# First layer of an MoE block on scaled fp16 pairs, with weight staging in freed slots and later maxima turns (one core)

## The chip, the cores and the metric

The kernel runs on one core of a Trainium2 chip. The metric is the time of one execution in microseconds (us) on the device. Engines: TensorE (PE) multiplies matrices, VectorE (DVE) and ScalarE (ACT) work elementwise, GpSimd (POOL) helps them, SyncE (SP) issues DMAs; GpSimd issues DMAs too.

## The reference

Causal attention with a bias from a cumulative sum gives x of 2304 tokens by 512; two mixture-of-experts blocks follow (as dense two-layer networks).

```
scores = q @ k.T / 8                       # 4 batches, 8 heads, 576 positions, 64 dims
bias   = min(-(cum_i - cum_j), 0),  cum = cumsum(max(s, 0))
x  = softmax(causal(scores + bias)) @ v    # -> (2304, 512)
h  = x @ moe_w_in                          # 512 x 2048
x  = (h * tanh(softplus(h))) @ moe_w_out   # 2048 x 512
h  = x @ moe2_w_in
out = (h * sigmoid(1.702 h)) @ moe2_w_out
```

## The kernel before

**Numbers in pairs.** A product of two float32 matrices is made of three matmuls (`mm3`): high by high, high by low and low by high part, since each operand is kept as a high part and the remainder. In the first block both parts are of the type fp32r, four bytes wide; in the second block they are fp16, scaled by powers of two.

**Weights.** The weights arrive as 64-bit numbers. For each of the 16 chunks (128 columns) of moe_w_in, `fetch_w` loads 512 KB into a staging tile `wst`; `turn_w` converts it: ScalarE once, VectorE twice (a shift, TENSOR_SCALAR, and a combination, SCALAR_TENSOR_TENSOR, both on 128x512 elements), then ScalarE copies the high part into `w` and GpSimd subtracts to get the low part.

**First layer (`first_layer`, `l1_mm`).** The 2304 tokens go in 9 units of 256 (`u`); each unit takes 16 chunks times 4 slices of 128 rows times 3 products, 192 matmuls of 128x256, into PSUM tile `h` (`acc` in the last two units); ScalarE evicts to `hs`, which goes to DRAM as `h_d`. Seven units are woven between attention steps (`slot_a`, `tick`), the last two stand behind the attention. x reaches this layer through `emit_tile`: TensorE transposes (`xt`), ScalarE writes the high part of `xh`, VectorE the low one.

**Start.** Up to step 6 of the attention the instructions stand in the order of the program (`nc.mode = "strict"`), with three calls of `bg_a` (one weight chunk each) between the scores of steps 3 to 5. Behind that a scheduler orders the instructions of each engine. Each engine then runs its own queue in order; the k, q and v loads stand in GpSimd's queue.

**Second layer.** The second layer of the first block goes over 5 spans of tokens (four of 512, one of 256), 960 matmuls `acc<-gh,w` and `acc<-gl,w`. After every 12 of these of 512 columns one background job (`bg_step`) is issued: passes over the second block's weights on VectorE (`out_pass1`, `out_scale`, `in_pass`, `in_split`, `in_scale`). The fourth span's matmuls are numbers 577 to 768.

**Maxima over the partitions (`across`).** For the scale of a span (`spx`) or of the weights (`gsc`) VectorE spreads a column over a 128x128 tile `bc`, TensorE transposes it into a bank of PSUM (`acc<-ident,bc` in the trace, "turn" below), and VectorE reduces it (`spx<-acc`, `gsc<-acc`). The turn is issued `wait` steps after the column; TensorE's next turn or matmul into the same bank waits for the reduce.

```
soon.append([wait, turn])
...
across(gsc[:, 0:1], out_scale2, 2 * SOON)      # SOON = 7
```

The second block starts at about 697 us, on fp16 pairs.

Of the kernel before, what the change touches and what calls it, by code (L numbers as in the profile page):

```python
# [19 lines left out]
VTOP = 16384.0  # L20
PH = 3
# [14 lines left out]
WAH = 1  # L36
LAG0 = 2
NEAR = 26
FA = 3
# [51 lines left out]
def attention_moe_moe_kernel(  # L91
# [82 lines left out]

    raw = {}
# [122 lines left out]

    vsc, vmx = {}, {}
# [14 lines left out]
    def vscale_set(b):  # L314
# [11 lines left out]
        nc.vector.tensor_scalar(out=t[:, 1:2], in0=t[:, 0:1], scalar1=PSC, scalar2=None, op0=ALU.mult)  # L326
# [287 lines left out]
    def norm_tile(x):  # L614
# [4 lines left out]
        nc.vector.tensor_scalar(out=rs, in0=su, scalar1=1e-9, scalar2=vsc[x["b"]][:, 1:2], op0=ALU.add, op1=ALU.mult)  # L619
# [3 lines left out]
    def emit_tile(x):  # L623
# [114 lines left out]
    I32 = mybir.dt.int32  # L738
# [32 lines left out]
    def turn_w(pool, lay, m, kind):  # L771
        t = pool.tile([128, 2, DM], F32R, tag="w", name="w")
        (win_t if kind == "in" else wout_t)[lay, m] = t
        r = fetched.pop((lay, m, kind))
        th, tl_ = t[:, 0, :], t[:, 1, :]
        if not wide:
            nc.scalar.activation(out=th, in_=r, func=AF.Copy)
            nc.vector.tensor_tensor(out=tl_, in0=r, in1=th, op=ALU.subtract)
            return
        zi, yi = r[:, :, 0], r[:, :, 1]  # L780
        y = yi.bitcast(F32)
        sided = lay == 0 and kind == "in"
# [12 lines left out]
        if lay == 0 and kind == "out":  # L795
            nc.gpsimd.tensor_scalar(out=th, in0=y, scalar1=1.0, scalar2=0.0, op0=ALU.mult, op1=ALU.add)
        else:
            nc.scalar.activation(out=th, in_=y, func=AF.Copy)
# [8 lines left out]
    def l1_mm(ps, lay, m, xr, first):  # L807
        w = win_t[lay, m]
# [7 lines left out]
    wq = list(range(NF))  # L816
# [50 lines left out]
    score(2)  # L867
    early_turn(1, 1)
# [5 lines left out]
    bg_a()  # L874
# [4 lines left out]
    bg_a()  # L879
# [3 lines left out]
    bg_a()  # L883
# [3 lines left out]
    emit_tile(steps[5])  # L887
    nc.mode = "after"
# [31 lines left out]

    def first_layer(u, xr, each):
        for m in range(0, NF, 4):
            t = tmp_pair(F32, "hs")
            for e in range(2):
                ps = ps_h.tile([128, 512], F32, tag="h", name="h")
                for d in range(2):
                    while wq and (0, min(NF - 1, m + 2 * e + d + WAH)) not in win_t:
                        bg_a()
                    while fq and fq[0] <= m + 2 * e + d + WAH + FA:
# [4 lines left out]
                nc.scalar.activation(out=o, in_=ps, func=AF.Copy)  # L934
# [91 lines left out]
    for m in range(NF):  # L1026
# [6 lines left out]
        nc.scalar.activation(out=o, in_=ps, func=AF.Copy)  # L1033
# [22 lines left out]
    def across(col, then, wait=SOON):  # L1056
# [9 lines left out]
        soon.append([wait, turn])  # L1066

    def soon_step():
        for x in soon:
            x[0] -= 1  # L1070
# [44 lines left out]
    def out_scale():  # L1115
        amax(gsc[:, 0:1], wom)
        across(gsc[:, 0:1], out_scale2, 2 * SOON)
# [109 lines left out]
    for i, (u, t0, W, m0, n) in enumerate(groups1):  # L1227
# [24 lines left out]
        if m0 + n == NF:  # L1252
# [3 lines left out]
            def out1(e, acc=acc, k_=k_, mx=mx, u=u, t0=t0, W=W):  # L1256
# [167 lines left out]
```

## Time and profile before

| | us |
|---|---|
| median of 3 runs | 1037.28 (1036.56 to 1040.79) |
| the profiled execution | 1039.73 |
| its span, first to last instruction | 1038.0 |
| TensorE busy | 985.0 (95%) |
| VectorE busy | 689.9 (66%) |
| ScalarE busy | 544.9 (52%) |
| GpSimd busy | 387.2 (37%) |

The span is the profiled execution without 1.7 us around it. Busy shares are means over stages: start to 49.6 us, first dense part to 109, a short part to 134.5 (the last step of batch 0), attention with the first layer to 420.4, second layer of the first block to about 697, then the second block. All instructions that a helper emits carry the line of that helper (L77), so that they are told apart by their tiles.

### The profile page before, as it was taken

The numbers are of one execution on the slowest core, as the hardware profiler recorded it, in microseconds if no ns is written. First come the engines' busy times: TensorE is split into PE (matmuls) and PEld (weight loads), VectorE is DVE, ScalarE is ACT, GpSimd is POOL, SyncE is SP. The second block draws the span as 40 slices with busy tenths as digits, with TensorE's granted clock in tenths as the row PEclk, the third lists the DMA queues.
The fourth block names the chain that finished last, engine by engine and source line by source line (L and its number), as shares of the span: only waits on it lengthen the run. The fifth ranks groups of instructions, "written<-read, shape, count | busy, mean of one in ns | idle before, by whom it ended". The sixth has DMA issues, their size and how long they took to land.

```text
span 1038.0 us, 20212 instructions
## 1 busy us (share of the span) xinstructions
PE 985.0 (95%) x7966; PEld 872.4 (84%) x7970; DVE 689.9 (66%) x1257; ACT 544.9 (52%) x1054; POOL 387.2 (37%) x414
## 2 busy tenths in 40 slices
PE   6799999989989899999996989999999999999997
PEld 5688798879979789998885868988888888888886
DVE  6478677755565775799998984985653653653553
ACT  4476577766665885365655564553433433333331
POOL 2544442243123311586321315575343442342431
PEclk9789999999999999999998999999999999999999
DMA  6458359997699978779996552600110100000000
GB/s 174 107 146 246 102 133 167 221 234 164 138 212 220 171 158 182 271 268 347 339 339 211 201 203 81 203 22 1 41 42 1 39 24 1 21 19 3 21 9 34
DMA packets 153775, 143.17 MB, mean 138 GB/s; under 512 B 91216, under 2 KB 122448, under 8 KB 153680
## 3 DMA queue, kind: packets, MB, share of 16 engines
q1 hardware_dynamic: 147456, 124.05, 43.9%
q0 software_dynamic: 6224, 17.83, 6.7%
q8 instruction: 62, 1.02, 0.4%
q14 instruction: 33, 0.27, 0.1%
HBM read 89.61 MB, written 32.58 MB: 118 GB/s over the span
## 4 chain that ended last, share of the span: by engine, by line
PE 48%; DVE 11%; DMA 10%; issue 3%; ACT 3%; POOL 2%; SPq 1%; DVEq 0%; ACTq 0%; POOLq 0%
PE h L77 24%; PE p L77 16%; DVE wst L77 5%; PE acc L77 4%; PE s L77 2%; DMA wst<-in_moe_w_out_dram 2%; DMA pt<-hl 2%; PE o L77 1%; DMA wst<-in_moe_w_in_dram 1%; DVE gl L77 1%; DMA vraw<-in_v_dram 1%; DMA h_d<-hs 1%; POOL w L77 1%; POOL w2d L77 1%; DMA w2f<-w_d 1%
## 5 line engine op out<-in xcount | busy, mean ns | idle before, releaser
L77 PE MATMUL h<-x,w2i 128*128 128x256 f16 x1728 | 200.0, 273 | 0.0
L77 PE MATMUL acc<-gh,w 128*128 128x512 f32 (+1 forms) x640 | 185.0, 374 | 13.5 <-DVE spx L77 13.5
L77 PE MATMUL h<-xh,w 128*128 128x256 f32 x1344 | 196.6, 295 | 1.1 <-ACT xh L77 0.7
L77 PEld LDWEIGHTS <-w2i 128*128 128x128 f16 x1728 | 169.0, 98 | 19.6
L77 PEld LDWEIGHTS h<-xh,w 128*128 128x128 f32 x1344 | 172.8, 195 | 4.1 <-ACT xh L77 1.1
L77 PEld LDWEIGHTS acc<-gh,w 128*128 128x128 f32 x640 | 117.9, 191 | 35.8 <-DVE spx L77 14.4
L77 PE MATMUL p<-w2h,gl 128*128 128x256 f16 x504 | 135.9, 273 | 1.1 <-DVE gl L77 1.1
L77 PE MATMUL p<-w2l,gh 128*128 128x256 f16 x504 | 136.0, 273 | 0.0
L77 PE MATMUL p<-w2h,gh 128*128 128x256 f16 x504 | 133.4, 273 | 1.1 <-ACT gh L77 0.9
L77 POOL TENSOR_TENSOR s<-z 128x256 f32<-128x256 f32 x72 | 54.7, 780 | 201.8 <-DVE z L77 201.8
L77 PE MATMUL acc<-gl,w 128*128 128x512 f32 (+1 forms) x320 | 119.2, 373 | 0.0
L77 PEld LDWEIGHTS <-gh 128*128 128x128 f16 x1008 | 98.5, 98 | 12.9 <-ACT gh L77 1.2
L77 ACT ACTIVATE sg<-h,spx 128x512 f32<-128x512 f32 x72 | 48.7, 680 | 105.0 <-PE h L77 105.0
L77 DVE TENSOR_TENSOR gl<-z,gh 128x768 f16<-128x768 f32 (+1 forms) x54 | 77.1, 1428 | 34.5 <-ACT gh L77 21.9
L77 DVE SCALAR_TENSOR_TENSOR wst<-wst 128x512 int32<-128x512 int32 x96 | 91.1, 958 | 10.0 <-ACT wst L77 6.6
L77 DVE SCALAR_TENSOR_TENSOR z<-h,sg 128x512 f32<-128x512 f32 x72 | 49.3, 687 | 68.8 <-ACT sg L77 68.7
L77 POOL TENSOR_TENSOR gl<-z,gh 128x1024 fp32r<-128x1024 f32 x18 | 51.0, 2832 | 116.9 <-ACT gh L77 103.8
L77 DVE TENSOR_TENSOR gl<-s,gh 128x1024 f16<-128x1024 f32 x36 | 44.2, 1228 | 68.5 <-ACT gh L77 68.5
L77 ACT ACTIVATE gh<-z 128x1024 fp32r<-128x1024 f32 (+1 forms) x72 | 67.9, 947 | 33.8 <-DVE z L77 29.4
L77 PE MATMUL s<-kw,qw 128*128 128x288 f32 (+4 forms) x352 | 81.8, 339 | 2.4 <-DVE kw L77 2.2
L77 ACT ACTIVATE gh<-s 128x1024 f16<-128x1024 f32 x36 | 38.0, 1057 | 81.7 <-POOL s L77 81.7
L77 ACT ACTIVATE P<-P,mx 128x128 f32<-128x128 f32 (+4 forms) x108 | 62.7, 582 | 19.9 <-DVE mx L77 19.5
(146 smaller groups left out, 1765.2 us busy)
## 6 DMA issues: line engine op xcount, KB each, us to landing
h_d<-hs SPq DMA_DIRECT2D x36, 512.0 KB, 4.4
hg<-h_d SPq DMA_DIRECT2D x36, 512.0 KB, 6.4
wst<-in_moe_w_in_dram SPq DMA_DIRECT2D x32, 512.0 KB, 5.3
wst<-in_moe_w_out_dram SPq DMA_DIRECT2D x32, 512.0 KB, 5.4
ck<-cum_d SPq DMA_DIRECT2D x6, 768.0 KB, 7.8
x_d<-x SPq DMA_DIRECT2D x18, 256.0 KB, 5.2
out_dram<-o SPq DMA_DIRECT2D x9, 512.0 KB, 2.8
kraw<-in_k_dram POOLq DMA_DIRECT2D x32, 128.0 KB, 4.1
```

Of the source, the lines that this page charges most:

```text
L77: r = f(*a, **kw)
```

## The change

The change has three parts.

First, the first layer's operands become scaled fp16 pairs. Two neighbouring chunks make a pair. `pair_a` converts both and takes their peaks on VectorE (`wmx`); `pair_b` makes one bound for the pair: `bound` spreads the peaks over the partitions by a TensorE matmul with ones into a tile `bd`, and VectorE reduces it, clamps, inverts and cuts it to a power of two (`wk`), with its inverse in `isw`. ScalarE writes the scaled high part, and VectorE (no longer GpSimd) the low part. x of batch 0 is scaled by a bound from the peaks of v (`v_peak`, `x_scale`); for later batches the power of two of v's scale stays in x. `evict` multiplies by the inverse scales in ScalarE's copy; at the borders of two batches (units 2, 4 and 6) it takes two copies in place of one, 24 more in all.

Second, chunks are staged in free slots of the 16 slots that the finished weights use (8 pairs, 8 stages), and fetched six chunks ahead (`FA`), no longer three.

Third, the turns of `out_scale` and of spans 0 to 2 are issued at steps 57, 59, 60 and 65 of a clock that counts all steps (`soon_step`), in place of 14 steps behind their columns. Of the 960 matmuls, 384, 468, 576, 732 and 768 stood in TensorE's queue ahead of the five turns before; now 648, 672, 694, 732 and 753 do, which is in the fourth span. The second and the later ones write into the bank that the turn ahead of them used.

```diff
-FA = 3
+FA = 6
...
+    def bound(t, cols, n, tiny, top):
+        ps = ps_s.tile([128, 512], F32, tag="s", name="bd")
+        nc.tensor.matmul(out=ps[:, 0:n], lhsT=ones, rhs=cols, start=True, stop=True, skip_group_check=True)
+        nc.vector.tensor_reduce(out=t, in_=ps[:, 0:n], axis=mybir.AxisListType.X, op=ALU.max)
+        nc.vector.tensor_scalar(out=t, in0=t, scalar1=tiny, scalar2=1.0 / top, op0=ALU.max, op1=ALU.mult)
+        nc.vector.reciprocal(t, t)
+        pow2(t)
...
+    def x_scale(k, ni):
+        for i in range(vmd[0], ni):
+            for g in range(2):
+                v_peak(i, g)
+        vmd[0] = max(vmd[0], ni)
+        sx[k] = t = sm_p.tile([128, 2], F32, tag="sx", name="sx", bufs=3)
+        bound(t[:, 0:1], vm0[:, 0:2 * ni], 2 * ni, 1.0e-30, VTOP)
+        ev_table(k, t)
+
+    def ev_table(k, t):
+        sx[k] = t
+        nc.vector.reciprocal(t[:, 1:2], t[:, 0:1])
...
-                xunit[u] = xh_a.tile([128, 2, KC, U], F32R, tag="xh", name="xh")
+                xunit[u] = xh_a.tile([128, 2, KC, U], F16, tag="xh", name="xh")
             xu = xunit[u]
             src = pv[:, :, done:done + m]
             hi = xu[:, 0, :, off:off + m]
-            nc.scalar.activation(out=hi, in_=src, func=AF.Copy)
-            nc.vector.tensor_tensor(out=xu[:, 1, :, off:off + m], in0=src, in1=hi, op=ALU.subtract)
+            lo = xu[:, 1, :, off:off + m]
+            if b:
+                nc.scalar.activation(out=hi, in_=src, func=AF.Copy)
+                nc.vector.tensor_tensor(out=lo, in0=src, in1=hi, op=ALU.subtract)
+            else:
+                k_ = f"u{u}"
+                if k_ not in sx:
+                    x_scale(k_, min(NTIL, (u + 1) * U // 128))
+                k_ = sx[k_][:, 0:1]
+                nc.scalar.activation(out=hi, in_=src, func=AF.Copy, scale=k_)
+                nc.vector.scalar_tensor_tensor(out=lo, in0=src, scalar=k_, in1=hi, op0=ALU.mult, op1=ALU.subtract)
             done += m
...
-            rt = tmp_pair(F32, "wst")
+            rt = wa_p.tile([128, 1024], F32, tag="w", name="wst")
...
+    def pair_a(p):
+        wmx[p] = t = sm_p.tile([128, 2], BF16, tag="wmx", name="wmx")
+        for m in (2 * p, 2 * p + 1):
+            while fq and fq[0] <= m:
+                fetch_a()
+            r = fetched[0, m, "in"]
+            y = to_f32(r, True) if wide else r
+            fetched[0, m, "in"] = y
+            peak(t[:, m % 2:m % 2 + 1], y)
+
+    def pair_b(p):
+        k = sm_p.tile([128, 1], F32, tag="wk", name="wk")
+        bound(k, wmx.pop(p), 2, TINY, WTOP1)
+        nc.vector.reciprocal(isw[:, p:p + 1], k)
+        win_t[p] = t = wa_p.tile([128, 2, 2, DM], F16, tag="w", name="w")
+        for e in range(2):
+            y = fetched.pop((0, 2 * p + e, "in"))
+            nc.scalar.activation(out=t[:, e, 0, :], in_=y, func=AF.Copy, scale=k)
+            nc.vector.scalar_tensor_tensor(
+                out=t[:, e, 1, :], in0=y, scalar=k, in1=t[:, e, 0, :], op0=ALU.mult, op1=ALU.subtract
+            )
...
+    def pairs_to(pa, pb):
+        for k, f, n in ((1, pair_b, pb), (0, pair_a, pa)):
+            while wq[k] < min(n, NF // 2):
+                f(wq[k])
+                wq[k] += 1
...
     early_pt(steps[2])
     early_av(steps[1])
-    bg_a()
     emit_tile(steps[1])
     score(4)
     early_pt(steps[3])
     early_av(steps[2])
-    bg_a()
+    pairs_to(1, 0)
     score(5)
     early_pt(steps[4])
     early_av(steps[3])
-    bg_a()
+    pairs_to(2, 1)
     early_pt(steps[5])
     early_av(steps[4])
     early_av(steps[5])
     emit_tile(steps[5])
+    pairs_to(2, 2)
...
+    def evict(o, ps, p, t0, t1, n):
+        ov, pv = (x.rearrange("p (d t) -> p d t", d=n) for x in (o, ps))
+        for a, z, k in x_class(t0, t1):
+            e = ev_need(k)[:, p:p + 1]
+            if k == "u0":
+                nc.vector.tensor_tensor(out=e, in0=isw[:, p:p + 1], in1=sx[k][:, 1:2], op=ALU.mult)
+            nc.scalar.activation(
+                out=ov[:, :, a - t0:z - t0], in_=pv[:, :, a - t0:z - t0], func=AF.Copy, scale=e
+            )
...
-                    while wq and (0, min(NF - 1, m + 2 * e + d + WAH)) not in win_t:
-                        bg_a()
-                    while fq and fq[0] <= m + 2 * e + d + WAH + FA:
+                    p = (m + 2 * e) // 2
+                    pairs_to(p + 2, p + 1 + d)
+                    while fq and fq[0] < m + 2 * e + d + FA:
                         fetch_a()
                     l1_mm(ps[:, d * U:(d + 1) * U], 0, m + 2 * e + d, xr, d == 0)
                     each()
                 o = t[:, e * 512:(e + 1) * 512]
-                nc.scalar.activation(out=o, in_=ps, func=AF.Copy)
+                evict(o, ps, m // 2 + e, u * U, (u + 1) * U, 2)
...
-        soon.append([wait, turn])
+        soon.append([wait - (clock[0] if wait > SOON else 0), turn])
+
+    clock = [0]
 
     def soon_step():
+        clock[0] += 1
...
-        across(gsc[:, 0:1], out_scale2, 2 * SOON)
+        across(gsc[:, 0:1], out_scale2, 57)
...
-                        spx[:, u, 0:1], lambda: span_scale(u) if ready[0] else waiting.append(u), 2 * SOON if u < 3 else 99
+                        spx[:, u, 0:1], lambda: span_scale(u) if ready[0] else waiting.append(u), (59, 60, 65, 999, 999)[u]
```

On **VectorE**, in the strict part at the start, before (`p` is a transposed block of probabilities, `x` the attention's output, `mx` and `rs` its maxima and sums):

```order
L77 TENSOR_REDUCE mx<-s 128x2
L77 COPY p_373<-pt 128x512
L77 TENSOR_SCALAR rs<-su 128x4
L77 RECIPROCAL rs<-rs 128x4
L77 TENSOR_TENSOR x<-o,rs 128x256
L77 TENSOR_SCALAR wst<-wst 128x512
L77 SCALAR_TENSOR_TENSOR wst<-wst 128x512
L77 COPY p_394<-pt 128x512
```

The same place after the change, up to the same copy (named p_430 here):

```order
L77 TENSOR_REDUCE wk<-bd 128x1
L77 TENSOR_SCALAR wk<-wk 128x1
L77 RECIPROCAL wk<-wk 128x1
L77 TENSOR_SCALAR wk<-wk 128x1
L77 RECIPROCAL isw<-wk 128x1
L77 SCALAR_TENSOR_TENSOR w<-wst,wk,w 128x512 x2
L77 TENSOR_SCALAR wst<-wst 128x512
L77 SCALAR_TENSOR_TENSOR wst<-wst 128x512
L77 TENSOR_REDUCE wmx<-wst 128x1
L77 TENSOR_SCALAR wst<-wst 128x512
L77 SCALAR_TENSOR_TENSOR wst<-wst 128x512
L77 TENSOR_REDUCE wmx<-wst 128x1
```

Where one conversion stood ahead of the copy, the bound and the low parts of the first pair and the conversion with peaks of the second pair stand now.

On **GpSimd**, the start of its queue, before:

```order
L77 MEMSET cumb 32x576
L77 TENSOR_TENSOR w<-wst,w 128x512 x3
L77 DMA kraw<-in_k_dram 128x4x64
L77 DMA qraw<-in_q_dram 128x4x64
L77 DMA v<-in_v_dram 128x4x64
L77 DMA kraw<-in_k_dram 128x4x64 x2
```

And after the change:

```order
L77 MEMSET cumb 32x576
L77 MEMSET vm_106 128x10
L77 MEMSET ones 128x128
L77 MEMSET maskp 128x64
L77 AFFINE_SELECT maskp<-maskp 64x64 x2
L77 DMA v<-in_v_dram 128x4x64 x4
L77 DMA v<-in_v_dram 64x4x64 x2
L77 DMA kraw<-in_k_dram 128x4x64
```

The three subtractions ahead of the loads are gone, and the v loads have moved ahead of the k loads.

On **VectorE** in the second layer, before, around the reduce of the second turn (`w2i` are the finished weights of the second block, `rk` their scales):

```order
L77 RECIPROCAL rk<-rk 128x1
L77 TENSOR_REDUCE mx_7265<-x_7266 128x1
L77 SCALAR_TENSOR_TENSOR w2i<-wst,rk,w2i 128x512 x2
L77 TENSOR_REDUCE spx<-acc 128x1
L77 SCALAR_TENSOR_TENSOR w2i<-wst,rk,w2i 128x512 x2
```

After the change, around the reduce of the first turn, which is behind the last pass over the weights:

```order
L77 TENSOR_REDUCE gsc<-rk 128x1
L77 SCALAR_TENSOR_TENSOR w2i<-wst,rk,w2i 128x512 x4
L77 COPY bc<-spx 128x128
L77 TENSOR_REDUCE gsc<-acc 128x1
L77 TENSOR_SCALAR gsc<-gsc 128x1
L77 RECIPROCAL gsc<-gsc 128x1
L77 TENSOR_TENSOR gl<-z,gh 128x1024
```

No reduce of a turn stands between the passes any longer; all of them follow the last split.

## Rows read from the trace of the kernel before

**Rows 1.** Busy time of each engine by stretch, with granted clock, DMA share and GB/s.
```profile
49.60:109.00 59.40, 55.72 (x414) 48.99 (x418) 47.27 (x91) 40.71 (x93) 26.80 (x27) 0.94 0.61 182
...
134.50:420.40 285.90, 271.88 (x2611) 247.81 (x2611) 184.50 (x502) 194.93 (x500) 75.53 (x106) 0.99 0.90 187
420.40:628.00 207.60, 194.05 (x988) 165.65 (x987) 191.84 (x259) 120.51 (x159) 87.60 (x49) 0.97 0.77 265
```

**Rows 2.** Timeline of VectorE, TensorE and GpSimd, 32 to 49 us.
```profile
32.77 0.68 DVE L77 COPY p<-pt 128x512 f32<-128x512 f32 x1
...
35.51 0.42 DVE L77 TENSOR_TENSOR x<-o,rs 128x256 f32<-128x256 f32 x1 [1.77 <-PE o L77]
...
37.37 7.47 PE L77 MATMUL h<-xh,w 128*128 128x256 f32 x36 [0.69 <-ACT xh L77]
...
48.75 0.62 PE L77 MATMUL s<-kw,qw 128*128 128x384 f32 x2 [2.16 <-DVE kw L77]
...
34.86 0.90 POOL L77 DMA_DIRECT2D kraw<-in_k_dram  x1
```

**Rows 3.** Groups of VectorE instructions up to 134.5 us (busy, mean ns, idle before).
```profile
L77 DVE SCALAR_TENSOR_TENSOR wst<-wst 128x512 int32<-128x512 int32 x16 | 11.7, 730 | 4.3 <-ACT wst L77 3.8
L77 DVE TENSOR_SCALAR wst<-wst 128x512 int32<-128x512 int32 x16 | 8.5, 533 | 0.1
...
L77 DVE TENSOR_REDUCE mx<-s 128x1 f32<-128x512 f32 x8 | 5.4, 679 | 0.3 <-PE s L77 0.3
...
L77 DVE TENSOR_TENSOR x<-o,rs 128x256 f32<-128x256 f32 x8 | 3.4, 422 | 2.1 <-PE o L77 1.8
...
L77 DVE RECIPROCAL rs<-rs 128x4 f32<-128x4 f32 x9 | 1.6, 173 | 0.2
```

**Rows 4.** VectorE timeline around 32 and 98 us: one step of the conversion.
```profile
31.64 0.42 DVE L77 TENSOR_SCALAR wst<-wst 128x512 int32<-128x512 int32 x1
32.16 0.69 DVE L77 SCALAR_TENSOR_TENSOR wst<-wst 128x512 int32<-128x512 int32 x1
...
98.74 1.19 DVE L77 TENSOR_SCALAR wst<-wst 128x512 int32<-128x512 int32 x1
```

**Rows 5.** Groups of GpSimd instructions up to 134.5 us.
```profile
L77 POOL TENSOR_TENSOR w<-wst,w 128x512 fp32r<-128x512 f32 x16 | 20.8, 1303 | 48.2 <-ACT w L77 47.4 <-issue 0.9
```

**Rows 6.** Chain of waits, 134.5 to 420.4 us: shares, and one piece.
```profile
by line: PE h L77 26.2%; PE s L77 8.8%; DMA pt<-hl 5.7%; PE o L77 5.3%; DMA vraw<-in_v_dram 3.8%; DMA vl<-in_v_dram 2.5%; DMA wst<-in_moe_w_out_dram 2.4%; issue 2.2%; DMA ck<-cum_d 2.2%; SPq L77 2.1%; PE kt L77 1.8%; PE qt L77 1.7%; DVE hl 
...
237.84 8.32 PE h L77 x69
```

**Rows 7.** Chain of waits, 697 to 1038 us: one piece.
```profile
700.58 2.62 PE h L77 x24
```

**Rows 8.** Groups of TensorE instructions, 134.5 to 420.4 us.
```profile
L77 PE MATMUL h<-xh,w 128*128 128x256 f32 x1115 | 158.9, 291 | 0.0
```

**Rows 9.** Groups of TensorE instructions, 420.4 to 628 us.
```profile
L77 PE MATMUL acc<-gh,w 128*128 128x512 f32 x443 | 140.5, 398 | 13.5 <-DVE spx L77 13.5
L77 PE MATMUL acc<-gl,w 128*128 128x512 f32 x221 | 87.6, 396 | 0.0
L77 PE MATMUL acc<-xh,w 128*128 128x256 f32 x321 | 38.7, 283 | 0.0
```

**Rows 10.** Waits of TensorE, 445 to 690 us.
```profile
PE acc L77 <- DVE spx L77: 13.5, 2, 9.6
```

**Rows 11.** The stretch behind the first turn, columns as in the first group.
```profile
561.00:565.75 4.75, 4.59 (x11) 3.63 (x12) 3.46 (x7) 2.02 (x4) 0.00 (x0) 0.50 0.83 251
```

**Rows 12.** VectorE timeline, late part.
```profile
560.82 0.28 DVE L77 TENSOR_REDUCE spx<-acc 128x1 f32<-128x128 f32 x1
...
622.86 4.31 DVE L77 SCALAR_TENSOR_TENSOR w2i<-wst,rk,w2i 128x512 f16<-128x512 f32 x4 [0.70 <-ACT w2i L77]
627.09 1.21 DVE L77 TENSOR_TENSOR gl<-z,gh 128x1024 fp32r<-128x1024 f32 x1
640.87 2.46 DVE L77 TENSOR_TENSOR gl<-z,gh 128x1024 fp32r<-128x1024 f32 x1 [12.56 <-PE acc L77]
```

More of the change, by code (lines that the diff above doesn't have):

```diff
@@ L20 @@
 VTOP = 16384.0
+WTOP1 = 16384.0
 PH = 3
@@ L172, in tmp_pair, with pow2, peak @@
         return p.tile([128, 1024], dt, tag="hs", name=nm)
+    I32 = mybir.dt.int32
+    def pow2(x):
+        nc.vector.tensor_scalar(
+            out=x.bitcast(I32), in0=x.bitcast(I32), scalar1=0x7F800000, scalar2=None, op0=ALU.bitwise_and
+        )
+    ones = const.tile([128, 128], BF16, name="ones")
+    isw = const.tile([128, NF // 2], F32, name="isw")
+    sx, evs = {}, {}
+    def peak(out, in_):
+        nc.vector.tensor_reduce(out=out, in_=in_, axis=mybir.AxisListType.X, op=ALU.max, apply_absolute_value=True)
+    def bound(t, cols, n, tiny, top):
[5 more added lines that the diff above has]
+        pow2(t)
     raw = {}
@@ L297, in split_items, with v_peak, ev_need, x_class @@
         return [qT], [v1, v2] if b else [], kT
+    vm0 = sm_p.tile([128, 2 * NTIL], BF16, tag="vm0", name="vm0", bufs=1)
+    vmd = [0]
+    def v_peak(i, g):
+        n = min(128, S - 128 * i)
+        peak(vm0[:n, 2 * i + g:2 * i + g + 1], vt[0, i, g][:n].rearrange("p h d -> p (h d)"))
+    def x_scale(k, ni):
[9 more added lines that the diff above has]
+        nc.vector.reciprocal(t[:, 1:2], t[:, 0:1])
+    def ev_need(k):
+        if k not in evs:
+            evs[k] = e = const.tile([128, NF // 2], F32, name=f"ev{k}")
+            if k != "u0":
+                nc.vector.tensor_scalar(out=e, in0=isw, scalar1=sx[k][:, 1:2], scalar2=None, op0=ALU.mult)
+        return evs[k]
+    def x_class(t0, t1):
+        r = []
+        while t0 < t1:
+            b = t0 // S
+            m = min(t1, (b + 1) * S)
+            r.append((t0, m, b if b else f"u{t0 // U}"))
+            t0 = m
+        return r
     vsc, vmx = {}, {}
@@ L325, in vscale_set @@
         nc.vector.reciprocal(t[:, 0:1], t[:, 0:1])
-        nc.vector.tensor_scalar(out=t[:, 1:2], in0=t[:, 0:1], scalar1=PSC, scalar2=None, op0=ALU.mult)
+        pow2(t[:, 0:1])
+        ev_table(b, t)
     LK = S // 128 * 128
@@ L618, in norm_tile @@
         su = ts["sums"]
-        nc.vector.tensor_scalar(out=rs, in0=su, scalar1=1e-9, scalar2=vsc[x["b"]][:, 1:2], op0=ALU.add, op1=ALU.mult)
+        nc.vector.tensor_scalar(out=rs, in0=su, scalar1=1e-9, scalar2=PSC, op0=ALU.add, op1=ALU.mult)
         nc.vector.reciprocal(rs, rs)
@@ L769, in fetch_w, with to_f32 @@
         fetched[lay, m, kind] = r
[L771 to L779, printed above, removed]
+    def to_f32(r, sided):
         zi, yi = r[:, :, 0], r[:, :, 1]
         y = yi.bitcast(F32)
-        sided = lay == 0 and kind == "in"
         if sided:
@@ L794, in turn_w @@
             )
[L795 to L798, printed above, removed]
+        return y
+    wmx = {}
+    def pair_a(p):
[18 more added lines that the diff above has]
+            )
+    def turn_w(pool, lay, m, kind):
+        t = pool.tile([128, 2, DM], F32R, tag="w", name="w")
+        wout_t[lay, m] = t
+        r = fetched.pop((lay, m, kind))
+        th, tl_ = t[:, 0, :], t[:, 1, :]
+        if not wide:
+            nc.scalar.activation(out=th, in_=r, func=AF.Copy)
+            nc.vector.tensor_tensor(out=tl_, in0=r, in1=th, op=ALU.subtract)
+            return
+        y = to_f32(r, False)
+        nc.gpsimd.tensor_scalar(out=th, in0=y, scalar1=1.0, scalar2=0.0, op0=ALU.mult, op1=ALU.add)
         nc.gpsimd.tensor_tensor(out=tl_, in0=y, in1=th, op=ALU.subtract)
@@ L815, in attention_moe_moe_kernel @@
     nxt = [0]
-    wq = list(range(NF))
+    wq = [0, 0]
     fq = list(range(NF))
@@ L844, in attention_moe_moe_kernel @@
     nc.gpsimd.memset(cumb[96:128], 0.0)
+    nc.gpsimd.memset(vm0, 0.0)
     nc.vector.tensor_copy(identb, ident)
+    nc.gpsimd.memset(ones, 1.0)
     one = sm_p.tile([128, H], F32, tag="one", name="one", bufs=1)
@@ L867, in attention_moe_moe_kernel @@
     score(2)
+    for i_, g in short:
+        v_peak(i_, g)
+    vmd[0] = 2
     early_turn(1, 1)
@@ L1032, in attention_moe_moe_kernel @@
             l1_mm(ps[:, d * U:(d + 1) * U], 0, m, xl[d], d == 0)
-        nc.scalar.activation(out=o, in_=ps, func=AF.Copy)
+        evict(o, ps, m // 2, (NU - UE) * U, NT, 1)
         if m % 2:
```

15 lines of the change are left out of this document (2 added, 13 removed).

## The prediction

> **What bounds the kernel now.** I read the busy time by stretch first [rows 1]; it shows no single bound. In the dense part from 49.6 to 109 us TensorE is busy 55.72 of 59.4 us, but VectorE has only 12.1 us free there. From 134.5 to 420.4 us TensorE leads (271.88 of 285.9). From 420.4 to 628 us VectorE is busy 191.84 of 207.6 us, and that is the stage where TensorE stands still: the table of waits has 13.5 us in two waits for `spx`, the longest 9.6 [rows 10]. To see whose the end of that stage is, I then followed VectorE's timeline: it goes through the passes over the second block's weights, starts the last split at 622.86 us, does a `gl` at 627.09 us, and then waits 12.56 us for TensorE [rows 12]. So VectorE's chain of passes ends at about 627 us, and from there the matmuls bound.
>
> **The change, step by step.**
>
> *Start, strict part.* Up to the copy of step 5's probabilities at 32.77 us [rows 2] VectorE gets: four peaks of v of 128x256, estimated from the 0.42 us of an operation of that size [rows 3], less overlap, at 0.37 each (1.5); one chunk's conversion more, by the starts of its two rows 0.52 + 0.61 [rows 4], 1.1; four peaks of 128x512, a 0.68 us reduce [rows 3] at the same spacing of 0.6 (2.4); one bound, five small operations at about 0.17 [rows 3] with starts 0.19 apart (0.95); two low parts at 0.61 (1.2). That is 7.1 us, less 0.3 for gaps that VectorE has there: +6.8. The first `h` matmul moves from 37.37 to about 44.2 us, and the scores of step 6, at 48.75 us [rows 2], to about 55.8. The `ones` matmul of a bound stands in TensorE's queue, so scores and transposes behind it wait for the peaks too; that is in these sums, since VectorE is the engine both wait for. GpSimd's queue no longer holds its loads behind three subtractions (k was issued at 34.86 us [rows 2]); that is worth nothing, since the k transposes stand behind the `h` matmuls on TensorE. Bounds: +3, if the first 36 matmuls (7.47 us, 207 ns each [rows 2]) run at the full-clock spacing of 120 ns instead, to +10, if the 12 more that now stand there run at 207 ns and one gap more opens.
>
> *Dense part to 109 us.* The added vector work is one peak and one low part of 128x512 for each of the remaining chunks, the bounds, and the scaled evictions' tables. Summed in the order of VectorE's queue with the durations above it goes from 41.4 to 59.1 us, +17.7. Against it stand 12.1 us in which VectorE is free [rows 1], so 5.6 at least don't fit. Some conversions get faster: the shift takes 0.42 us alone [rows 4], but 0.53 on the mean of 16 [rows 3] and 1.19 in a place [rows 4], and the combination 0.73 on the mean against 0.69 alone; GpSimd's 16 subtractions of 1.30 us [rows 5] go away, and if they cause all of it, 16 x (0.11 + 0.04) = 2.4 us come back. The Trainium skill (GPSIMD Engine Reference, Specifications) says that GpSimd shares SBUF interfaces with VectorE and contends with it for some of its modes; the slow rows fit, but by that page alone no sum follows. I take +4: 5.6 less the relief, plus a little of the free time that can't be used. Bounds: +3 and +8, if half the free time stays, and +17.7 if it all does.
>
> *fp16 in place of fp32r, attention stage.* In a run of 69 an fp32r matmul of 256 columns takes 8.32/69 = 120.6 ns [rows 6]; in the second block, the same shape on fp16 takes 2.62/24 = 109.2 ns [rows 7]. So 11.4 ns of each could go. 1115 of them lie in the stage [rows 8], 12.7 us if all counted. But `h` holds only 26.2% of the stage's chain [rows 6], 74.9 us, and 9.45% of that is 7.1. I take -8, nearer to the chain than to the count, since a shorter run lets some more through. Bounds: -12.7, and -4 if half of the shortening turns into waits for DMA, which is 0.90 busy there [rows 1] (`pt<-hl` alone is 5.7% of the chain [rows 6]). The 24 added ScalarE copies and the small `ev` operations lie beside 91 us of free ScalarE and 101 us of free VectorE [rows 1] and cost nothing; if that cover were gone, 24 x 0.6 = 14 us would be at stake. The Trainium skill (TensorE: Matmul & The Clock Gate, Back-to-back issue gap) gives a warm gap of columns over 2.4 GHz plus 2.5 ns, 109 ns for 256 columns, and names no type; by that rule the old matmuls would be at 109 too and this term 0. The rows show 120.6 for fp32r, and they decide.
>
> *Fetching six ahead, staging in freed slots.* TensorE shows no wait for a first-layer weight load to be removed, and the bytes are the same: 0.
>
> *Last two units.* 386 matmuls there (321 of them behind 420.4 us [rows 9]) would be 4.4 us shorter. VectorE's chain of passes, which starts at 420 us, ends the stage, so this is hidden.
>
> *The turns.* Both waits of TensorE, 13.5 us [rows 10], go away, and the slow restart behind each: 4.75 us at a granted clock of 0.50 behind the first [rows 11], 2.4 us lost, and by estimate the same again behind the second. 18 us, then, in which TensorE gets ahead. But at 628 us it had done 664 of the 960 matmuls [rows 9], and the second turn now stands behind number 672. It needs the bank of the first turn, whose reduce stands in VectorE's queue directly behind the last split, at about 627 us as before, since VectorE has the same passes (16 splits, 80 and 48 conversion steps, 16 `gl`) ahead of it. So TensorE waits there, with 288 matmuls left behind it instead of 296: 8 x 0.227 = 1.8 us gained, and about 2 us lost as it restarts after the wait at half clock. The stall isn't removed but gathered in one place: 0. Behind the waiting turn stand all matmuls of the fourth span, and `gl` on VectorE waits for those. Bounds: -22 (13.5 + 4.4 + 4.4, if VectorE doesn't bind) and +2.
>
> **Sum.** 6.8 + 4 - 8 + 0 = +2.8 us. On the profiled execution, 1039.73 us, this is 1042.5. That execution was 2.45 us above the median of 1037.28, so on the scale of the median it is 1040.
>
> **The rivals.**
> *A (my forecast)*, about 1040, its own range 1034 to 1047 by the start's +3 to +10 and the gain's -4 to -12.7.
> *B, the vector work comes in series.* The free time of VectorE in the dense part is waiting for ScalarE and TensorE in a fixed order, and stays; +17.7 in place of +4, and the fp16 gain only -4 because of the DMA: 6.8 + 17.7 - 4 = +20.5 at the worst. Half way there, +15, it gives 1052. For it: queues are in order, and peak, bound, copy and low part follow each other across three engines. Against: the scheduler knows the new operations and can fill. It decides from the point where less than half of the 12.1 us is filled.
> *C, VectorE does not bind the second layer.* Its 15.8 free us there [rows 1] shrink when the turns' reduces go, and TensorE, 18 us ahead, lets `gl` start earlier. Then 13 to 22 us are won: 1040 - 18 = 1022. For it: TensorE's restart closes the chain at the second turn before. Against: VectorE was free for 15.8 us of 207.6 only, and the last split is ahead of the first reduce.
> *D, the early work is covered.* The dense part costs +1 and the fp16 gain is whole, -12.7, the start +3: -8.7, 1029. For it: GpSimd's 20.8 us of subtractions [rows 5] vanish, and 1115 matmuls do get shorter. Against: `h` is a quarter of the chain only.
>
> **Numbers.** Chances: A 0.49, B 0.19, C 0.17, D 0.15. The range leaves out the far half of C and of B: 1024 to 1051. A difference of 0.5%, 5.2 us, is about what a measurement of this kernel can tell from none: faster, below 1032.1, is D and C, 0.32 in all; slower, above 1042.5, is B and the upper quarter of A, 0.31; the rest 0.37.
>
> **What the profile after would show.** The first `h` matmul at 43 to 45 us if the start is right; the end of batch 0 (the first `P<-s,ck`, at 134.5 us now) 8 to 14 us later, 20 or more for B; fp16 `h` runs at 109 ns each; the stage from there to the last attention output shorter by 6 to 10 us; one wait of TensorE of 12 to 18 us for a `gsc` reduce at about matmul 672, and VectorE at the last split again some 207 us behind its first pass. C is right if TensorE waits less than 5 us in the second layer. The prediction is wrong as a whole if VectorE's passes end earlier, measured from their start, or if the dense part grows by over 10 us.

## The result and the profile after

The changed kernel is slower: its time stands to that of before as 1.0075, with a 95% interval of 1.0051 to 1.0100, which is 7.8 us of 1038 (5.3 to 10.4). The medians of 19 runs each are 1047.39 and 1037.79 us. The ratio leaves out runs more than 1.5% above the fastest of their kernel, five of the changed kernel's 19, which the medians, 9.6 us apart, count. The runs of the changed kernel scatter more, from 1036 to 1059 us. The profiled execution took 1044.33 us, its span is 1042.6, 4.6 us more than before; the terms below are made on spans of profiles, and the scatter counts against each of them.

Most of that scatter is TensorE's granted clock. Time multiplied by mean granted clock is an estimate of what a run would take if all of it were at 2.4 GHz and bound by TensorE; the rest of the time is then what the lower clock costs, at most. Over the 19 runs of the changed kernel the product of span and clock stays between 1008.7 and 1020.2 us (mean 1012.7), and the rest goes from 22.8 to 42.3 us (mean 33.3). In 25 runs of the kernel before, taken beside later runs, the means are 1014.7 and 22.4 us. By this estimate the work became 2 us shorter, and the whole loss is time at the lower clock.

Busy time by stretch of the changed kernel, cut at four events: the scores of step 6, the first `P<-s,ck` of VectorE (end of batch 0), the first conversion of the second block, the end of its last split (columns as in [rows 1]):

```profile
0.00:56.15 56.15, 36.63 (x228) 29.09 (x228) 37.64 (x92) 22.23 (x62) 16.76 (x36) 0.85 0.51 137
56.15:155.52 99.37, 87.08 (x615) 69.52 (x619) 76.59 (x196) 54.01 (x126) 19.89 (x27) 0.88 0.43 128
155.52:430.30 274.78, 254.34 (x2610) 215.45 (x2609) 187.58 (x512) 200.63 (x524) 76.08 (x106) 0.99 0.91 194
430.30:631.80 201.50, 190.07 (x996) 158.56 (x994) 185.84 (x248) 123.06 (x159) 88.02 (x49) 0.98 0.79 273
631.80:1042.60 410.80, 402.89 (x3534) 360.29 (x3534) 227.00 (x323) 155.87 (x209) 170.30 (x182) 0.99 0.10 35
```

The kernel before, cut at the same two events where [rows 1] was cut otherwise, and at the end of its last split:

```profile
48.75:134.48 85.73, 81.66 (x619) 69.62 (x624) 61.56 (x130) 53.37 (x128) 36.97 (x41) 0.96 0.53 155
...
420.40:627.10 206.70, 193.15 (x984) 164.91 (x983) 190.94 (x259) 120.51 (x159) 87.60 (x49) 0.97 0.77 265
627.10:1038.00 410.90, 402.45 (x3546) 360.22 (x3544) 226.66 (x313) 155.59 (x209) 166.95 (x182) 0.99 0.10 35
```

| stage | before | after | difference | forecast |
|---|---|---|---|---|
| to the scores of step 6 | 48.75 | 56.15 | +7.4 | +6.8 |
| rest of batch 0 | 85.7 | 99.4 | +13.6 | +4 |
| attention with the first layer | 285.9 | 274.8 | -11.1 | -8 |
| second layer to the last split | 206.7 | 201.5 | -5.2 | 0 |
| the rest | 410.9 | 410.8 | -0.1 | 0 |

The largest miss is the second row. There VectorE is busy 76.59 us, 15.0 more than before, but TensorE's granted clock also fell on the mean from 0.96 to 0.88. Where it fell, in stretches of the changed kernel:

```profile
60.00:64.00 4.00, 2.05 (x15) 1.36 (x14) 3.91 (x8) 1.32 (x3) 1.51 (x3) 1.00 0.99 284
64.00:75.00 11.00, 8.96 (x42) 7.81 (x42) 7.83 (x19) 6.58 (x16) 1.66 (x3) 0.53 0.50 136
75.00:93.00 18.00, 16.14 (x135) 13.46 (x134) 17.78 (x46) 11.46 (x26) 0.82 (x2) 1.00 0.25 67
93.00:102.00 9.00, 8.07 (x41) 6.03 (x41) 7.67 (x22) 5.64 (x11) 0.00 (x0) 0.62 1.05 352
116.00:127.50 11.50, 9.02 (x52) 7.51 (x53) 10.99 (x36) 4.71 (x10) 3.86 (x5) 0.70 0.19 52
```

Between 60 and 64 us VectorE is busy 3.91 of 4 us and TensorE 2.05; behind that TensorE runs at the lower of its two levels, 1.2 GHz, until 75 us. The timeline of TensorE has a wait ahead of the first such stretch, the longest inside it, the last ahead of the second and the longest ahead of the third:

```profile
63.77 0.62 PE L77 MATMUL s<-kw,qw 128*128 128x384 f32 x2 [1.24 <-DVE kw L77]
...
66.69 1.11 PE L77 MATMUL kt<-ident,kraw 128*128 128x128 f32 x4 [2.04 <-ACT P L77]
...
94.45 0.18 PE L77 MATMUL bd<-wmx,ones 128*128 128x2 bf16 x1 [0.84 <-DVE wk L77]
...
117.52 0.66 PE L77 MATMUL pt<-ident,P 128*128 128x128 f32 x4 [2.58 <-DVE p L77]
```

Before, only one such stretch lay behind the scores of step 6, at 50 to 57 us; after, there are three (64 to 75, 95 to 102, 119 to 126). The new work by group, up to the end of batch 0, and the two conversion steps, which answer to [rows 3]:

```profile
L77 DVE SCALAR_TENSOR_TENSOR w<-wst,wk,w 128x512 f16<-128x512 f32 x16 | 11.7, 744 | 1.2 <-ACT w L77 1.2
L77 DVE SCALAR_TENSOR_TENSOR wst<-wst 128x512 int32<-128x512 int32 x16 | 10.9, 685 | 0.8 <-ACT wst L77 0.5
L77 DVE TENSOR_REDUCE wmx<-wst 128x1 bf16<-128x512 f32 x16 | 10.9, 682 | 0.2
...
L77 DVE TENSOR_SCALAR wst<-wst 128x512 int32<-128x512 int32 x16 | 6.7, 438 | 0.1
...
L77 DVE TENSOR_REDUCE vm<-v 128x1 bf16<-128x256 f32 x8 | 2.8, 414 | 0.0
```

In the second layer TensorE's table of waits, 445 to 690 us, which answers to [rows 10], has the two waits for `spx` gone and one for the reduce of the first turn in their place:

```profile
PE acc L77 <- DVE gsc L77: 8.0, 1, 8.0
PE acc L77 <- ACT x L77: 3.7, 1, 3.7
```

### The profile page after: what moved, and what is told of

It is laid out like the page before. It is cut to its first block, busy times and chain, and to the rows that moved or that the text cites. A ratio compares the mean times of both kernels' runs of the same rounds, so it can differ in the third digit from the quotient of the medians.

```text
span 1042.6 us, 20336 instructions
## 1 busy us (share of the span) xinstructions
PE 971.0 (93%) x7978; PEld 832.9 (80%) x7981; DVE 714.7 (69%) x1370; ACT 555.8 (53%) x1078; POOL 371.0 (36%) x400
## 4 chain that ended last, share of the span: by engine, by line
PE 32%; DVE 11%; issue 6%; DMA 5%; POOL 3%; ACT 2%; SPq 1%; DVEq 0%; ACTq 0%; POOLq 0%
PE h L77 17%; PE p L77 16%; DVE wst L77 6%; DMA wst<-in_moe_w_in_dram 2%; POOL w2d L77 2%; DMA wst<-in_moe_w_out_dram 1%; DVE gl L77 1%; DMA h_d<-hs 1%; DVE mx L77 1%; DVE wim L77 1%; SPq L77 1%; DMA w_d<-w2y 1%; DVE w2l L77 1%; POOL gl L77 1%; DMA x<-x_d 1%
## 5 line engine op out<-in xcount | busy, mean ns | idle before, releaser
L77 PEld LDWEIGHTS <-w 128*128 128x128 f16 x1728 | 167.3, 100 | 25.1 <-issue 3.0
L77 PE MATMUL h<-xh,w 128*128 128x256 f16 x1344 | 173.5, 279 | 1.9 <-DVE xh L77 1.1
L77 PEld LDWEIGHTS <-gh 128*128 128x128 f16 x1008 | 98.5, 98 | 12.3 <-ACT gh L77 0.6
L77 PE MATMUL s<-kw,qw 128*128 128x288 f32 (+4 forms) x352 | 87.5, 355 | 4.3 <-DVE kw L77 2.9
L77 DVE SCALAR_TENSOR_TENSOR wst<-wst 128x512 int32<-128x512 int32 x96 | 88.3, 928 | 4.3 <-ACT wst L77 1.6
```

The costliest lines, as they stand in the source:

```text
L77: r = f(*a, **kw)
```

## The experiments

Two theories stood at first for the loss in batch 0. S: the added VectorE work stands in series, some 0.8 us of time for each us of work. L: the handovers between engines count, not the amount.

**Peaks taken twice.**

```
             peak(t[:, m % 2:m % 2 + 1], y)
+            peak(t[:, m % 2:m % 2 + 1], y)
```

> The changed kernel with each of the 16 peaks of the weights taken twice, nothing else. Theory S (the added VectorE work stands in series with the rest of batch 0): 16 x 0.6 = 9.6 us more VectorE work, of which about 0.8 shows, so the end of batch 0 moves from 155.5 to about 163 us and the time by +8. Rival L (the loss comes from the lock-step of peak, ones-matmul, bound, copy and low part across engines, not from the amount of work): no new handover, so the end of batch 0 stays within 2 us of 155.5.

End of batch 0 at 158.28 us (changed kernel 155.52 and, in a second profile, 157.14); time 1.0123 of before (1.0091 to 1.0155), an interval that overlaps that of the changed kernel. S, with 0.8 us per us, asked for 163 us, and L for at most 157.5: neither came, but this end of batch 0 is one profile, and another profile of the changed kernel's instructions (the run with the old turns below) ends batch 0 at 150.39 us, so it refutes neither firmly. VectorE did 6 us more work in the same stretch, and the mean clock is higher:

```profile
58.68:158.28 99.60, 86.34 (x618) 66.62 (x619) 82.61 (x208) 53.92 (x126) 19.89 (x27) 0.91 0.43 128
```

**A constant scale for the weights, low part on VectorE.**

```
-            peak(t[:, m % 2:m % 2 + 1], y)
...
-        bound(k, wmx.pop(p), 2, TINY, WTOP1)
-        nc.vector.reciprocal(isw[:, p:p + 1], k)
+        k = kc[:, 0:1]          # 65536.0
```

> The changed kernel with a constant scale of 65536 for the weights in place of the bound from their peaks: the 16 peaks, the 8 ones-matmuls and the 40 small operations are left out, the low part stays on VectorE. S: 16 x 0.6 + 8 x 0.95 = 17 us less VectorE work, 0.8 of it seen: end of batch 0 at about 142 us, time 13 to 14 us below the changed kernel. L: the handovers through TensorE are gone too, so the end of batch 0 comes at 137 us or earlier although the low parts (10 us) still stand on VectorE.

End of batch 0 at 138.99 us, between the two; 0.9923 of before (0.9888 to 0.9959), faster than both kernels. The rest of batch 0 takes 12 us less than in the changed kernel, with 10.6 us less VectorE work, and the clock is back at 0.96; one stretch at half clock is left, at 61 to 68 us:

```profile
51.83:138.99 87.16, 79.25 (x614) 62.67 (x613) 65.95 (x148) 52.93 (x126) 19.88 (x27) 0.96 0.49 146
```

**The same with the low part on GpSimd**, as before the change: the scale folded into the first conversion step, then a plain subtraction.

```
+            held(lut(y, y, AF.Prelu, scale=2.0 ** -110, alpha=-(2.0 ** 32)))     # 2.0 ** -112 before
...
-            nc.vector.scalar_tensor_tensor(out=t[:, e, 1, :], in0=y, scalar=k, in1=t[:, e, 0, :], ...)
+            nc.gpsimd.tensor_tensor(out=t[:, e, 1, :], in0=y, in1=t[:, e, 0, :], op=ALU.subtract)
```

> As the run with the constant scale, with the scale folded into the first conversion step and the low part subtracted by GpSimd as before the change. VectorE then has no added work for the weights. S: end of batch 0 at 136 to 140 us (134.5 before, plus the peaks of v, less what fp16 saves), time about 1028 to 1031, faster than the kernel before by 7 to 10 us. L with the clock as cause: the same place as the run with the low part on VectorE, since the handovers are the same there.

Both missed: end of batch 0 at 146.47 us, time 1.0000 of before (0.9966 to 1.0034), though VectorE has the least work of all variants of the changed kernel. TensorE waits 6.34 us for k in one place:

```profile
63.22 1.97 PE L77 MATMUL kt<-ident,kraw 128*128 128x128 f32 x8 [6.34 <-ACT kraw L77]
```

The loads of k stand in GpSimd's queue. Its timeline has them behind the subtractions, which wait for `w` until 42.87 us; three loads of k are issued from 53.71 us in this run:

```profile
42.87 2.26 POOL L77 TENSOR_TENSOR w<-wst,w 128x512 f16<-128x512 f32 x2 [6.27 <-ACT w L77]
45.08 0.90 POOL L77 DMA_DIRECT2D kraw<-in_k_dram  x1
...
49.75 3.47 POOL L77 DMA_DIRECT2D v<-in_v_dram  x5
53.21 0.56 POOL L77 TENSOR_SCALAR_AFFINE_SELECT maskp<-maskp 64x64 bf16<-64x64 bf16 x2
53.71 2.26 POOL L77 DMA_DIRECT2D kraw<-in_k_dram  x3
```

and from 48.90 us with the low part on VectorE:

```profile
48.90 2.22 POOL L77 DMA_DIRECT2D kraw<-in_k_dram  x3 [29.21 <-PE kt L77]
```

So freeing GpSimd's queue is worth something to this kernel when the pairs are fp16: there the first loads are issued from 13.56 us. A run with the subtractions moved behind the loads was not tried.

**The changed kernel once more.**

> The changed kernel once more, unchanged, to see which stage its scatter (1036 to 1059 us) comes from. S: the end of batch 0 again at 155 us within 3, and the stages behind it within 2 us of the first profile, so that the scatter lies in batch 0. Rival: batch 0 is the same and the stages behind differ by 5 us or more.

Stages of 57.5, 99.7, 278.1 and 205.8 us: the end of batch 0 repeats within 1.6 us, the attention is 3.3 and the second layer 4.3 us longer than in the first profile. Between these two profiles the scatter lies behind batch 0 more than in it, as the rival has it. Two profiles are too few: with the third one of the same instructions, from the run with the old turns, the end of batch 0 scatters by 6.7 us (150.39 to 157.14). Time 1.0101 (1.0041 to 1.0161).

With that a third theory, W: waits of TensorE bring a stretch at half clock behind them, which is paid in addition to the work.

**Peaks alone** (the run with the constant scale, its peaks put back and read by nobody):

```
+            peak(t[:, m % 2:m % 2 + 1], y)   # result unused
```

> The run with the constant scale with its 16 peaks put back, which nothing reads: 16 x 0.6 = 9.6 us of VectorE work without a bound behind it. Theory W (each TensorE wait for VectorE of about 2 us or more in batch 0 brings a stretch at half clock behind it, so what counts is how many such waits there are): end of batch 0 at 141 to 149 us with one or two stretches at half clock after 49 us. Theory S (VectorE's work in series): 139.0 + 0.8 x 9.6 = 147 us with the granted clock of the dense part at 0.96 as without the peaks. If the bounds alone matter: 139 to 141 us.

**Bounds alone** (no peaks; the bound is taken of a constant):

```
-            peak(t[:, m % 2:m % 2 + 1], y)
...
-        bound(k, wmx.pop(p), 2, TINY, WTOP1)
+        bound(k, kc, 2, TINY, WTOP1)          # kc holds 0.25
```

> The changed kernel with its 16 peaks of the weights left out, and the bounds taken of constants instead, with the same ones-matmul and the same five small operations of VectorE. W: the small operations are 0.15 us each but stand scattered between others, and ScalarE's scaled copy waits for the last; if the chain through three engines makes the waits, the end of batch 0 comes at 148 us or later, with two stretches at half clock or more. S: 139.0 + 0.8 x 7.6 = 145 us, clock 0.96.

End of batch 0 at 145.49 us with the peaks, 146.27 us with the bounds, against 138.99 with neither and 150.39, 155.52 or 157.14 with both: 6.5 and 7.3, together 11.4 to 18.2. So it is not shown that the two together cost more than their sum. Times 1.0026 (1.0006 to 1.0046) and 1.0006 (0.9975 to 1.0036). With the peaks one half-clock stretch is left (64 to 71 us), with the bounds two (62 to 69 and 110 to 117 us), as W has it, but the bounds came below the 148 us of W, and the peaks' clock of 0.96 is what S said. Neither theory fits alone. The rest of batch 0 with peaks alone:

```profile
54.86:145.49 90.63, 80.37 (x614) 62.84 (x613) 72.45 (x160) 52.85 (x126) 19.88 (x27) 0.96 0.48 139
```

and with bounds alone:

```profile
54.28:146.27 91.99, 82.85 (x618) 65.20 (x619) 69.58 (x185) 53.60 (x126) 19.89 (x27) 0.93 0.46 139
```

Put side by side, time multiplied by mean granted clock (the estimate of the section on the result; the clock has two digits, so a row is good to 0.5 us) separates the two parts. Two rows are of runs told further below:

| rest of batch 0 | us | clock | us x clock | lost to the clock | VectorE busy |
|---|---|---|---|---|---|
| neither | 87.16 | 0.96 | 83.7 | 3.5 | 65.95 |
| bounds | 91.99 | 0.93 | 85.6 | 6.4 | 69.58 |
| peaks | 90.63 | 0.96 | 87.0 | 3.6 | 72.45 |
| both (changed kernel) | 99.37 | 0.88 | 87.4 | 11.9 | 76.59 |
| both, with the old turns | 95.36 | 0.93 | 88.7 | 6.7 | 76.17 |
| peaks twice | 99.60 | 0.91 | 90.6 | 9.0 | 82.61 |
| both, fetching three ahead | 105.44 | 0.84 | 88.6 | 16.9 | 78.95 |
| kernel before | 85.73 | 0.96 | 82.3 | 3.4 | 61.56 |

The fourth column follows VectorE's work: from "neither" to "peaks twice" 6.9 us for 16.7, some 0.4 us for each us. The fifth does not; "peaks twice" and "both" have three stretches at half clock each, but 17.1 and 23.9 us in sum.

The two rows of "both" test W. Up to the end of batch 0 the old turns change nothing: the instructions of VectorE, ScalarE and GpSimd are the same in number and order, and TensorE's waits behind the scores of step 6 sum to 12.3 and 12.8 us. Yet one profile has three stretches at half clock with 23.9 us, the other two with 13.7 us (63 to 70 and 114 to 121), and it is 4.0 us shorter. So with the same work and equal waits, 10.2 us more at half clock go with 4.0 us more time. But W does not hold as it stands: equal waits did not bring equal stretches. In the ten us ahead of the second stretch above no wait is longer than 0.84 us; that wait stands in the other profile too, and the clock did not fall there:

```profile
92.30 0.18 PE L77 MATMUL bd<-wmx,ones 128*128 128x2 bf16 x1 [0.83 <-DVE wk L77]
```

What decides whether a stretch comes stays open.

**The old turns in the changed kernel.**

```
-        across(gsc[:, 0:1], out_scale2, 57)              # and (59, 60, 65, 999, 999)[u]
+        across(gsc[:, 0:1], out_scale2, 2 * SOON)        # and 2 * SOON if u < 3 else 99
```

> The changed kernel with the turns 14 steps behind their columns, as before the change. My forecast (the stall is only gathered at the last split): time within 3 us of the changed kernel, two TensorE waits for spx of 13 us in sum again, VectorE's passes from first to last split 200 to 207 us. Rival (the early turns free TensorE): 5 us or more slower than the changed kernel in the second layer.

1.0071 (1.0048 to 1.0095): the time doesn't tell it from the changed kernel. In the profile the waits for `spx` are back, 19.1 us in two, and the second layer to the last split takes 207.5 us, 6.0 and 1.7 more than in the two profiles of the changed kernel. Batch 0, which the edit doesn't touch, ends 5 to 7 us earlier than there and hides it:

```profile
55.03:150.39 95.36, 82.74 (x618) 65.65 (x619) 76.17 (x196) 54.01 (x126) 19.90 (x27) 0.93 0.44 134
```

**The new turns in the kernel before.** The same edit the other way round.

> The kernel before with the new turns alone. My forecast: 0 within 2 us of the kernel before; one wait for a gsc reduce of 10 to 18 us at matmul 672 takes the place of the two. Rival: the passes of VectorE get shorter by some 5 us, as from 206 to 201 us in the changed kernel, and the time falls by 4 to 5 us. If it is not this, the shorter passes come from fp16 in the last two units.

0.9964 (0.9944 to 0.9983), 3.7 us faster (1.8 to 5.8): nearer to the rival than to the forecast. TensorE's waits in the second layer, then the stretches before and behind the last split:

```profile
PE acc L77 <- DVE gsc L77: 9.2, 1, 9.2
```

```profile
415.80:618.90 203.10, 192.70 (x1002) 165.22 (x1000) 186.88 (x248) 121.29 (x160) 88.54 (x49) 0.99 0.77 271
618.90:1030.00 411.10, 402.27 (x3534) 359.80 (x3534) 230.23 (x324) 154.97 (x209) 167.62 (x182) 0.99 0.10 35
```

One profile would not show 3.6 us in a stage (its attention stage, which the edit doesn't touch, is 4.4 us shorter than before). But in all eleven profiles with the new turns the second layer takes 201.5 to 205.8 us to the last split, in the two with the old ones 206.7 and 207.5.

**Both scales constant.** As the run with the weights' scale constant, with x of batch 0 scaled by a constant as well.

```
-        for i in range(vmd[0], ni): ... v_peak(i, g)
-        bound(t[:, 0:1], vm0[:, 0:2 * ni], 2 * ni, 1.0e-30, VTOP)
-        ev_table(k, t)
+        sx[k] = kx                   # 16384 and its inverse, set once
```

> The constant scale for the weights, and for x of batch 0 a constant of 16384 too: the ten peaks of v, their bounds and the tables made from them are left out as well, so that both scales rest on knowing the size of the inputs. What is left of the change is fp16 itself, the low part on VectorE and the later turns. Theory W: the first h matmul at about 39.5 us, the scores of step 6 at 49 to 50, end of batch 0 at 135 to 137 us; time 1027 to 1029 us, faster than the kernel before by 1%. Rival (the start is fixed by the weights' conversion alone): no difference from the run with the weights' scale alone constant, 1031 us.

1029.26 us, 0.9910 (0.9883 to 0.9937), some 9 us below the kernel before: the lowest median here. The scores of step 6 come at 48.68 us, end of batch 0 is 134.19 us, as before the change. The interval overlaps that of the weights' constant alone, so by time the two are not told apart; the start, 3.2 us earlier, tells them apart in the profile.

**Two products instead of three in the first layer** (the lines shortened).

```
-            mm3(ps, hi_w, lo_w, xr(0, c), xr(1, c), ...)
+            matmul(ps, hi_w, xr(0, c)); matmul(ps, hi_w, xr(1, c))
```

> The changed kernel with the third product of the first layer (low weight by high x) left out: 576 matmuls of 256 columns less, 448 of them before the last two units. My forecast's view (h is a quarter of the chain of the attention stage, 275 us with about 1100 h matmuls): a third less, 370 x 0.109 = 40 us of TensorE work, of which a quarter to a third shows, so the stage takes 262 to 266 us and the waits for pt<-hl grow from 15 to 30 us or more. Rival (TensorE's work sets the stage): 235 to 240 us.

One run. The attention stage takes 267.7 us, 7 to 10 less than in the changed kernel's two profiles, for 26 us less of busy TensorE; the 262 to 266 us expected were just missed, and so were waits for `pt<-hl` of 30 us or more. The stage and its waits for the transposed probabilities (total, times, longest):

```profile
152.56:420.30 267.74, 227.99 (x2191) 188.02 (x2189) 188.48 (x515) 201.09 (x525) 76.06 (x107) 0.90 0.94 199
```

```profile
PE o L77 <- DMA pt<-hl: 25.0, 19, 3.7
```

The DMA engines are busy 0.94 of the time, and the clock is down to 0.90. The waits for `pt<-hl` are 9.7 us longer than in the changed kernel. By the estimate used above the lower clock costs 27 us of this stage (0.10 of it), against 3 there, so more of the saving went there than into the waits: at full clock the stage would be near 241 us, against 272. The rival's time of 235 to 240 us did not come; its premise, that TensorE's work sets the stage, is not refuted for the full clock.

**Fetching three ahead in the changed kernel.**

```
-FA = 6
+FA = 3
```

> The changed kernel with chunks fetched three ahead in place of six. My forecast: fetching ahead is worth 0, so the end of batch 0 stays at 155 to 158 us and the time within 4 us of the changed kernel. Rival: late weights make TensorE wait for the first conversion step, and the end of batch 0 comes 5 us or more later.

1.0178 (1.0152 to 1.0204), end of batch 0 at 162.74 us, and TensorE waits 5.1 us for `wmx` in two places: the rival is right. The rest of batch 0 has 2.4 us more VectorE work than in the changed kernel, but 34 us at half clock in four stretches, and is 6.1 us longer, 5.0 of it by the clock in the estimate:

```profile
57.30:162.74 105.44, 91.94 (x618) 72.30 (x619) 78.95 (x196) 53.78 (x126) 19.89 (x27) 0.84 0.43 131
```

The old condition, with its own extra chunk and a "not greater", fetched five chunks, so this run goes below the kernel before and isn't an undo of the change; it shows that the new pairs need the distance.

## Why the forecast came out as it did

The range (1024 to 1051) held the measured 1047.39. The forecast of 1040 was 7 us short, and the sign of the result, slower by more than 0.5%, had a chance of 0.31. Single terms were off by more than their sum, and against each other: +9.6 us in batch 0 behind the start, -3.1 in the attention, -5.2 in the second layer, by the first profile. That the time still fell into the range is luck. The prediction named two signs of being wrong as a whole, that VectorE's passes end earlier from their start, or that the dense part grows by over 10 us. Both came: 201.5 us instead of 207, and +13.6 (+9.6 in the run with the old turns). Of its other signs the 109 ns of a fp16 matmul held; batch 0 ended 21.0 us later (8 to 14 expected, 20 or more for B), and the one wait for `gsc` was 8.0 us (12 to 18).

Some of its sums are off, though none moves the forecast: by its own terms the low end of A is 1031.6 and not 1034, half way from A to B is +11.7 and not +15, the last two units have 384 matmuls and not 386, and the bound of -22 takes 4.4 us for a restart that its own row prices at 2.4.

*Start, +6.8: right.* +7.4 in the first profile, +8.7 in the second, +6.3 in the run with the old turns. The first `h` matmul came at 45.51 us (44.2 forecast); dropping the peaks and bounds of the weights moved it to 41.81, and those of v as well to 39.76 us. The shown cause is the one named: added work of VectorE in a fixed order.

*Dense part, +4: the step that failed.* It was sized as "5.6 less the relief, plus a little of the free time that can't be used", a balance of VectorE's work against its free time. Measured are +13.6. By the table, 5.1 of them are work (87.4 against 82.3), near the term, and 8.5 are time at half clock (11.9 against 3.4), which the sum did not have at all. It had priced such a loss behind the two turns [rows 11] but not here, where [rows 1] has a clock of 0.94 and TensorE was about to get new waits. The run with the old turns, with the same instructions in batch 0, splits otherwise: 6.4 us of work and 3.3 of clock. The rival B gave the right sign, and by its own test it even looks right: VectorE's free time in this stretch was 24.2 us before and 22.8 after. But by the estimate at full clock the added work costs 0.4 us for 1 us, not the whole of it; much of the free time after is time that the half clock added. That peaks and bounds bring the half clock is shown (two of the three stretches vanish when they go). That it is TensorE's waits is argued: a wait without added VectorE work came in twice, 6.34 us for k with GpSimd's subtractions, with 13.7 us at half clock instead of 6.8, and 5.1 us for `wmx` with three chunks ahead, with 34 instead of 23.9; but equal waits gave 23.9 us in one profile and 13.7 in another.

*GpSimd's relief.* The forecast allowed 2.4 us for faster conversion steps; the means went from 533 to 438 and from 730 to 685 ns, 16 x 0.14 = 2.2 us. The trace agrees with the contention that the Trainium skill names (GPSIMD Engine Reference, Specifications) for the first of the two: with the subtractions put back on GpSimd its mean was 507 ns, against 424 without them. The second stayed (689 against 692), so what shortened it is open. "Worth nothing", said of GpSimd's freed queue, was wrong at least in the presence of fp16: the run with GpSimd's subtractions put back lost 7.5 us in batch 0 to the run without.

*fp16, -8: right in the profile, too large on the mean.* -11.1 in the first profile, -7.8 in the second, and 274.8 to 285.2 us (mean 279.6) over ten profiles of fp16 variants with all three products against 285.9 and 281.5 on fp32r: -4, the bound that the forecast set for the least gain. The price of one matmul was right: the starts of `h` matmuls in a run are 109 ns apart at the median, 120 before. Their row, which answers to [rows 8], and the waits for `pt<-hl` in the stage, before and after:

```profile
L77 PE MATMUL h<-xh,w 128*128 128x256 f16 x1115 | 140.9, 275 | 0.7 <-DVE xh L77 0.7
...
PE o L77 <- DMA pt<-hl: 7.3, 6, 2.3
...
PE o L77 <- DMA pt<-hl: 15.3, 11, 3.1
```

The row is busy 18.0 us less, and the waits grew by 8 us: part of the shortening turned into waits for DMA, as that bound had it. What it did not have is the clock: by the same estimate as above, at full clock, the ten profiles are at 268 to 275 us (mean 271.7) and the two on fp32r at 282.5 and 278.1, which is the forecast's -8; the half clock takes 3 to 12 us in the ten and 3.4 in the two.

*Last two units, 0, and the turns, 0.* The gathering of the stall was right, its size not: one wait of 8.0 us (9.2 in the kernel before with new turns) for the `gsc` reduce behind the last split, where 12 to 18 were expected. The step that failed is that VectorE's last split ends "at about 627 us as before, since VectorE has the same passes": the passes themselves got shorter, 203.1 us with the new turns alone against 206.7, and the turns are worth 3.7 us. With fp16 and the new turns the passes take 201.5 to 205.8 us, with fp16 and the old ones 207.5, so the shorter matmuls of the last two units are not the cause and are hidden, as forecast. Of the 3.6 us, 2.2 are eleven small operations of the maxima that stood on VectorE ahead of the last split and stand behind it now: three reduces of turns (one took 0.28 us [rows 12]), three copies into `bc`, five operations on `gsc`. The sum of passes left them out. The rest, 1.4 us, is within the scatter of the stage.

*Fetching ahead, 0: not shown.* The run with three ahead says that distance matters; what the step from five to six is worth was not tried.

## What to carry to other kernels

When work is added to an engine that others wait for, its free time in the profile says whether the work fits, but not what TensorE's clock does: here 7 to 17 us more at half clock came with it in three profiles, which by the estimate cost 3.3 to 8.6 us beside 5.1 to 6.4 us of work. Put each run's granted clock beside its time before explaining a scatter. Look for the cheapest form of a bound before costing a cheaper matmul: the change paid only when the peaks and bounds of the weights were gone (0.992; 0.991 with those of v gone too, of which the later turns alone give 0.996), and that needs inputs whose size is known. And when a stage's DMA engines are nine tenths busy, shorter matmuls can come out as longer waits and as time at half clock.

## What was not expected of the hardware

Granted clock and VectorE's work came apart: with the peaks taken twice the stretch had 6 us more VectorE work and yet a higher mean clock (0.91 against 0.88) and the same length. And the same instructions of batch 0 took 95.4 us in one profile and 99.4 in another behind the scores of step 6, with almost equal waits of TensorE; 13.7 and 23.9 us of that were at half clock. Leaving out a third of the first layer's products, 26 us of busy TensorE, shortened the attention stage by 7 to 10 us only, with the clock down from 0.99 to 0.90.
